# Attention and experts in one Trainium2 kernel: V loaded per quad, K's copy on VectorE, score steps in halves, one PV group per quad, gate by one matmul

## Chip, cores, metric

The kernel runs on one core of one Trainium2 chip. The metric is the device time in microseconds, median of the runs. On one core a run counts as slow when it is over 1.5% above the fastest run of the same kernel. A **ratio** below is the mean time of one kernel's fast runs over the mean of the other's fast runs of the same rounds on the same chip, with a 95% interval, so it is not quite the ratio of the medians quoted beside it.

## The reference, cut

```
q, k, v: [8 batches, 8 heads, 576, 64]   f: [8, 8, 576]
scores = q k^T / 8 + decay from cumsum(log f), causal
x = softmax(scores) v                     -> [8, 576, 512]
e = argmax(mean_over_positions(x) @ w_gate)          # one expert per batch
out = gate * (relu(x @ w1[e]) @ w2[e])               # w1, w2 fp32 in memory, 2 MB each per expert
```

## The kernel before

Four heads of a batch are a **quad** (16 quads), and a quad's scores are made in four **slots**. A slot is one call of `stage_s`: matmuls into four banks of PSUM, the memory that matmuls write (one bank per head), one exponential on ScalarE (ACT) over all four, and a mask on GpSimd (POOL). `stage_pv` makes row sums (`r_ps`) and outputs (`o_ps`), and VectorE (DVE) scales them into `xT`. Reading a result out of PSUM, which frees its tile for the next matmuls, is called an **eviction** below. When both quads of a batch are done, `stage_gate` picks the expert, `stage_weights` loads its weights from POOL's queue, and the expert matmuls are fed in between the slots by `moe(...)`. They start at slot 14. Every engine works through its instructions in the order they are written here.

```
ps_s: one tile [P, 4, 512] fp32 (4 PSUM banks);  ps_w: 4 tiles of one bank, shared by
row sums, outputs, gate and both expert stages

def stage_t(g, j):                       # j = 0: Q, 1: K
    nc.vector.transpose(TR[j], RAW...)
    if j == 0: nc.vector.tensor_copy(dst, src)
    else:      nc.gpsimd.tensor_copy(...)          # K's copy on POOL
def stage_s(g, k):
    ps = ps_s.tile([P, 4, 512], fp32, name="s_ps")
    ... matmuls of 4 heads (4 row groups of the array) into ps[:, j, ...]
    nc.scalar.activation(E[:, :, 0:WIDTH[k]], ps[:, :, 0:WIDTH[k]], AF.Exp, scale=0.125)
    ... nc.gpsimd.affine_select(...)               # mask
def stage_pv(g, blk):                    # 3 tiles of ps_w: r_ps, o_ps, o_ps
    ...
    if n == 1 and blk == 1: nc.vector.tensor_add(pt, pooled[:, :, 0], pooled[:, :, 1])
def stage_gate(b):
    for m in range(4):
        nc.tensor.matmul(lg_ps, pt[:, m:m + 1].to_broadcast([P, P]), wg[:, m, :], start=(m == 0), stop=(m == 3))
    ... logits, max, index, exponential
# ... cut ...
for t in range(4 * NQ + 2):
    g, k4 = divmod(t, 4)
    if g < NQ: stage_s(g, k4)
    # ... t == 0 cut
    if k4 == 0:   moe(t, 0.5); stage_pv(g - 1, 1); ... load_v(batch g // 2 + 1); moe(t, 0.5)
    elif k4 == 1: stage_v(g + 1); stage_t(g + 1, 0); moe(t, 1.0); stage_gate; stage_weights; moe(t, 1.2)
    elif k4 == 2: moe(t, 1.0); stage_pv(g, 0); stage_t(g + 1, 1); moe(t, 0.9)
    else:         load_qk(g + 3, ...); moe(t, 2.4)
```

The softmax here doesn't subtract the row's maximum and nothing guards it: scores larger than these inputs give would overflow.

## Time and profile before

| | before |
|---|---|
| median of 3 runs | 264.78 us (263.08 to 269.06; the last counts as slow) |
| span of the profiled run | 261.2 us |
| first score matmul | 11.35 us |
| first expert matmul | 56.1 us |
| last matmul ends | 255.6 us |

From the page: busy share of each engine, and the granted clock of the matmul engine (PE) in tenths, in 40 slices of 6.5 us.

```profile
PE 224.3 (86%) x3202; PEld 151.7 (58%) x3218; DVE 126.8 (49%) x352; ACT 155.3 (59%) x216; POOL 131.0 (50%) x166
...
PE   6256565569999898999999999999999999999991
...
PEclk9655557579999999999999999999999999999999
```

The clock is at 0.5 to 0.7 from the second to the ninth slice (about 6 to 59 us) and full after that. The same cut by the two borders of the table (columns: stretch, its length, busy time of PE, weight loads, VectorE, ScalarE, POOL, then PE's granted clock, the share of DMA time, GB/s):

```profile
11.35:56.10 44.75, 25.84 (x482) 15.97 (x482) 15.47 (x45) 27.28 (x34) 29.13 (x36) 0.58 0.85 159
56.10:255.60 199.50, 194.20 (x2708) 134.28 (x2724) 104.82 (x290) 125.70 (x180) 97.44 (x120) 0.99 0.84 182
```

I call 11.35 to 56.1 us the **fill** and 56.1 to 255.6 the **full part**. In the fill no engine is busy for more than about two thirds of the time. In the full part PE is busy 194.2 of 199.5 us, so every microsecond of PE work or of PE waiting there is a microsecond of the kernel. Who PE waited for, whole run (total us, times, longest):

```profile
PE s_ps L177 <- POOL kt L169: 14.4, 8, 5.6
PE s_ps L177 <- ACT E L184: 10.7, 11, 2.0
```

The two large waits are nearly all in the fill (12.8 and 10.2 us of them): K's copy on POOL, and the exponential that must empty the four score banks first. And the gate's matmuls, from the costliest groups (busy us, mean ns):

```profile
L241 PE MATMUL logits_ps<-wg,pooledT 128*128 128x8 f32 x64 | 7.8, 248 | 0.4 <-DVE pooledT L234 0.2
```

Their 64 records are eight gates; merged in time each gate keeps PE for 0.8 to 1.0 us.

### The profile page before, as it was taken

Reading aid. Unit: us, or ns where it says so; the run is one execution under the profiler, and the core shown is the slowest. Engines: PE = TensorE matmul, PEld = TensorE weight load, DVE = VectorE, ACT = ScalarE, POOL = GpSimd, SP = SyncE. Lnnn points to the kernel's source line nnn. Section 1 sums busy time; section 2 is a strip of 40 time slices with the busy share of each in tenths; the row PEclk is TensorE's granted clock in tenths of the full one; section 3 lists DMA queues with packets and bytes.
Section 4 is the critical chain, followed back from the end, with each engine's and each line's share of the span. In section 5 each row is a group of like instructions: output and inputs, shape, how many; then the busy total and the mean of one; then the engine's idle time right before and its main releaser. Section 6 shows DMA issues by size and latency. Waiting matters only on the chain.

```text
span 261.2 us, 7676 instructions
## 1 busy us (share of the span) xinstructions
PE 224.3 (86%) x3202; PEld 151.7 (58%) x3218; DVE 126.8 (49%) x352; ACT 155.3 (59%) x216; POOL 131.0 (50%) x166
## 2 busy tenths in 40 slices
PE   6256565569999898999999999999999999999991
PEld 2133333337855684578656865587548755976940
DVE  4551325035645564556554645565646534544430
ACT  3175648357756876678667876688568864430500
POOL 4389564854576557374856584758545621100000
PEclk9655557579999999999999999999999999999999
DMA  6998932999369998999699989999990594299132
GB/s 131 227 231 148 197 52 54 212 218 174 75 123 242 251 229 142 224 277 231 105 229 244 250 159 224 267 218 163 224 262 26 93 221 153 52 191 244 62 101 89
DMA packets 51865, 45.82 MB, mean 175 GB/s; under 512 B 39344, under 2 KB 40624, under 8 KB 50800
## 3 DMA queue, kind: packets, MB, share of 16 engines
q0 software_dynamic: 7936, 26.22, 53.8%
q1 hardware_dynamic: 43456, 18.39, 28.1%
q8 instruction: 27, 0.44, 0.7%
q10 hardware_dynamic: 432, 0.66, 0.7%
q14 instruction: 14, 0.11, 0.1%
HBM read 62.03 MB, written 9.44 MB: 274 GB/s over the span
## 4 chain that ended last, share of the span: by engine, by line
PE 51%; ACT 14%; DVE 12%; DMA 8%; POOL 7%; issue 6%; POOLq 0%; SPq 0%; ACTq 0%; DVEq 0%
PE h_ps L277 17%; PE out_ps L292 16%; ACT E L184 9%; PE s_ps L177 7%; PE o_ps L220 5%; DMA w1e<-in_moe_w_dram 4%; POOL kt L169 4%; DVE tr L162 4%; DMA out_dram<-otile 3%; PE r_ps L220 3%; PE out_ps L305 3%; DVE xT L228 2%; POOL vb L155 2%; ACT ri L226 2%; ACT h1T L283 1%
## 5 line engine op out<-in xcount | busy, mean ns | idle before, releaser
L184 ACT ACTIVATE E<-s_ps 128x1536 bf16<-128x1536 f32 x64 | 96.2, 1503 | 48.8 <-PE s_ps L177 47.8
L277 PE MATMUL h_ps<-xT,w1e 128*128 128x288 bf16 x512 | 73.7, 292 | 2.2 <-ACT h1T L283 1.1
L277 PEld LDWEIGHTS <-w1e 128*128 128x128 bf16 x512 | 62.5, 146 | 9.1 <-issue 5.9
L228 DVE SCALAR_TENSOR_TENSOR xT<-o_ps,ri 128x256 bf16<-128x256 f32 (+1 forms) x64 | 27.0, 456 | 66.9 <-ACT ri L226 59.8
L177 PE MATMUL s_ps<-qt,kt 32*128 32x320 bf16 (+4 forms) x896 | 37.7, 281 | 25.0 <-POOL kt L169 14.4
L292 PE MATMUL out_ps<-w2e,h1T 128*128 128x512 bf16 x240 | 57.9, 380 | 1.0 <-issue 0.3
L283 ACT ACTIVATE h1T<-h_ps,gate_b 128x288 bf16<-128x288 f32 x64 | 31.8, 497 | 27.3 <-PE h_ps L277 27.3
L177 PEld LDWEIGHTS <-kt 32*128 32x128 bf16 x896 | 19.9, 97 | 44.8 <-issue 20.5
L196 POOL TENSOR_SCALAR_AFFINE_SELECT E<-E 128x512 bf16<-128x512 bf16 x32 | 20.8, 649 | 43.2 <-ACT E L184 43.1
L155 POOL TENSOR_TENSOR vb<-vf,WF 128x1024 bf16<-128x1024 f32 (+1 forms) x32 | 40.5, 1266 | 1.3
L292 PEld LDWEIGHTS <-h1T 128*128 128x128 bf16 x256 | 23.2, 98 | 28.9 <-issue 3.5
L280 DVE TENSOR_SCALAR h1T<-h_ps,gate_b 128x288 bf16<-128x288 f32 x64 | 31.8, 508 | 14.4 <-PE h_ps L277 14.4
L299 DVE COPY otile<-out_ps 128x512 f32<-128x512 f32 x31 | 21.3, 688 | 27.2 <-PE out_ps L292 26.7
L220 PE MATMUL o_ps<-E,vb 128*32 128x320 bf16 (+4 forms) x896 | 31.6, 286 | 0.0
L169 POOL COPY kt<-tr 128x576 f32<-128x576 f32 x16 | 20.2, 1260 | 20.5 <-DVE tr L162 19.4
L187 POOL TENSOR_SCALAR_AFFINE_SELECT E<-E 128x1024 bf16<-128x1024 bf16 x16 | 17.4, 1089 | 15.1 <-ACT E L184 15.1
L162 DVE STREAM_TRANSPOSE tr<-raw 128x576 f32<-128x576 f32 x32 | 24.7, 772 | 0.0
L220 PEld LDWEIGHTS <-vb 128*32 128x32 bf16 x896 | 21.8, 107 | 4.5
L220 PE MATMUL r_ps<-E,WB 128*32 128x320 bf16 (+4 forms) x448 | 19.2, 289 | 0.9 <-POOL E L196 0.9
L224 ACT ACTIVATE lr<-r_ps 128x256 f32<-128x256 f32 (+1 forms) x32 | 13.1, 410 | 7.5 <-PE r_ps L220 7.4
L220 PEld LDWEIGHTS <-WB 128*32 128x32 bf16 x448 | 9.6, 100 | 9.7 <-issue 6.3
L226 ACT ACTIVATE ri<-lr 128x256 f32<-128x256 f32 (+1 forms) x32 | 14.2, 445 | 1.0
(52 smaller groups left out, 115.1 us busy)
## 6 DMA issues: line engine op xcount, KB each, us to landing
vf<-in_v_dram SPq DMA_DIRECT2D x32, 256.0 KB, 7.7
w1e<-in_moe_w_dram POOLq DMA_DIRECT2D x8, 1024.0 KB, 8.2
w2e<-in_moe_w_dram POOLq DMA_DIRECT2D x8, 1024.0 KB, 13.4
out_dram<-otile SPq DMA_DIRECT2D x29, 256.0 KB, 6.8
raw<-in_q_dram POOLq DMA_DIRECT2D x16, 288.0 KB, 6.7
raw<-in_k_dram POOLq DMA_DIRECT2D x16, 288.0 KB, 7.8
vf<-in_v_dram SPq DMA_DIRECT2D x8, 128.0 KB, 6.9
out_dram<-otile SPq DMA_DIRECT2D x16, 64.0 KB, 7.5
```

The source lines that it names most:

```text
L155: nc.gpsimd.tensor_tensor(VB[g % NV][p0:P, c0:c1, :, :], VF[b % 2][p0:P, c0:c1, h, :], WF[p0:P, b, c0:c1, h].unsqueeze(3).to_broadcast([P ...
L162: nc.vector.transpose(TR[j], RAW[g % NRAW][:, j, :, :].rearrange("p r e -> p (r e)").bitcast(fp32))
L169: nc.gpsimd.tensor_copy(dst.rearrange("p i r -> p r i"), TR[j].rearrange("p (r i) -> p r i", r=18))
L177: nc.tensor.matmul(ps[:, j, at:at + hi - lo], KT[g % 2][32 * j:32 * j + 32, KLO[c]:KLO[c] + P, a], QT[g % 2][32 * j:32 * j + 32, lo:hi, a] ...
L184: nc.scalar.activation(E[:, :, 0:WIDTH[k]], ps[:, :, 0:WIDTH[k]], AF.Exp, scale=0.125)
L220: nc.tensor.matmul(ps[32 * j:32 * j + 32, lo - i0:w], lhs, E[:, j, at:at + i1 - lo], start=(m == 0), stop=(m == len(segs) - 1))
L228: nc.vector.scalar_tensor_tensor(xT[:, 2 * n + what - 1, i0:i1], ps[:, 0:w], LN_SCALE, ri[:, 0:w], op0=ALU.mult, op1=ALU.mult, accum_out=p ...
L277: nc.tensor.matmul(p1[:, 0:288], w1e[:, m, s:FH:8], xT[:, m, s0:s0 + 288], start=(m == 0), stop=(m == 3))
L280: nc.vector.tensor_scalar(h1T[:, s, s0:s0 + 288], p1[:, 0:288], gate_b[:, 0:1], 0.0, op0=ALU.mult, op1=ALU.max)
L283: nc.scalar.activation(h1T[:, s, s0:s0 + 288], p1[:, 0:288], AF.Relu, scale=gate_b[:, 0:1])
L292: nc.tensor.matmul(p2, h1T[:, hb, s0:s0 + 128], w2e[:, hb, :], start=(hb == 0), stop=(hb == 7))
L299: nc.vector.tensor_copy(otile, p2)
```

## The change

The intent: shorten the fill, and take work off PE in the full part. It loads V per quad instead of per batch; copies K on VectorE and issues the transposes earlier; in the first 14 slots (`FILL`) splits a score step into two halves of two heads, so that one half's exponential can run beside the other half's matmuls; adds two dummy matmuls per slot there to hold the clock up; joins the two PV blocks into one group per quad; makes the gate by a product and a sum on VectorE and one matmul; moves the cumulative sum's tail to POOL. Core of the diff, cuts marked:

```
+    FILL = 14
+    SPS = ps_s.tile([P, 4, 512], fp32, name="s_ps")          # one tile for the whole run
# ... V tiles and loads per quad, cumulative sum on gpsimd: cut ...
-        if j == 0:
-            nc.vector.tensor_copy(dst, src)
-        else:
-            nc.gpsimd.tensor_copy(...)
+        nc.vector.tensor_copy(dst, src)
     def stage_s(g, k):
-        ps = ps_s.tile([P, 4, 512], fp32, name="s_ps")
-        ...
-        nc.scalar.activation(E[:, :, 0:WIDTH[k]], ps[:, :, 0:WIDTH[k]], AF.Exp, scale=0.125)
+        for heads in (((0, 1), (2, 3)) if 4 * g + k < FILL else ((0, 1, 2, 3),)):
+            ... matmuls of these heads into SPS[:, j, at:at + hi - lo]
+            h = slice(heads[0], heads[-1] + 1)
+            nc.scalar.activation(E[:, h, 0:w], SPS[:, h, 0:w], AF.Exp, scale=0.125)
-    def stage_pv(g, blk):
+    def stage_pv(parts):
+        for what, g, blk in [(0, g, blk) for g, blk in parts] + [(w, g, blk) for g, blk in parts for w in (1, 2)]:
     def stage_gate(b):
-        for m in range(4):
-            nc.tensor.matmul(lg_ps, pt[:, m:m + 1].to_broadcast([P, P]), wg[:, m, :], ...)
+        nc.vector.tensor_tensor(prod, wg..., pt..., op=ALU.mult)
+        nc.vector.tensor_reduce(part, prod, axis=X, op=ALU.add)
+        nc.tensor.matmul(lg_ps, ones, part)
# the loop, new order inside a slot:
+        if parts and not fill: stage_pv(parts)                # slot 1: (g-1, 1) and (g, 0)
+        if gate and not fill:  stage_gate(...); stage_weights(...)      # slot 2
+        if g < NQ: stage_s(g, k4)
+        if gate and fill:      stage_gate(...); stage_weights(...)
+        if g < NQ: stage_mask(g, k4)
+        if parts and fill:     stage_pv(parts)
+        # slot 1: stage_t(g+1, 0), load_v(g+2);  slot 2: load_qk(g+3), stage_v(g+1), stage_t(g+1, 1)
+        moe(t, (1.4, 2.2, 2.2, 2.1)[k4])
+        if fill: busy(2)                                       # dummy matmuls
```

## The prediction

> **What bounds it now.** By the windows view the kernel has two parts. From 12 to 56 us (score steps before the first expert matmul) PE is busy about 57% at a granted clock near 0.5; no engine is full there (ACT about 62%). From 70 to 213 us PE is busy 138.2 of 143 us at clock 1.00: PE-bound, with only 4.8 us of idle left. The tail (213 to 255) is pure expert matmul, also full, then about 6 us for the last store.
>
> In the fill a quad takes about 12.5 us. The chain of waits shows why it is serial: scores (0.85 us) then one exponential over four PSUM banks (1.24 to 1.88 us), each waiting for the other; xT, then the K transpose on DVE (0.77), then K's copy on POOL (1.26), and only then the next quad's scores. The timeline of POOL shows that copy queued behind V scaling (2.59 us) and masks; PE waits 2.9 to 4.3 us for it at 35.2 and 48.7 us. The first expert index is ready at about 41.7 us, but POOL issues the weight load at 45.67, after a mask and V scaling; w1e lands 10.4 us later and expert work starts at 56.1.
>
> **Costed.**
> - K's copy on DVE: about 0.7 us instead of 1.26 on POOL, both transposes emitted a slot or more earlier. Removes the waits of 2.9 to 5.6 us at quad starts in the fill; in the full part only 0.2 to 0.3 us per quad. DVE +10 us, POOL -20 us; neither is full. The Trainium skill ("SBUF — State Buffer", shared port pair) says VectorE and GpSimd exclude each other in some modes; the trace agrees (one Q copy took 1.56 instead of 0.65 us beside V scaling), so a few copies will be long.
> - Half steps: exponentials cost about 0.165 us + 0.84 ns per element (from 1.24, 1.45, 1.88 us), so a quad's rise from 6.0 to 6.7 us of ACT; with 1.7 us for Ln/Exp of the sums, 8.4 us if ACT never waits. I estimate 9.3 us per quad, as the six-tile PV group in four PSUM buffers waits for Ln on ACT.
> - Dummy matmuls keep PE warm. The skill ("TensorE: Matmul & The Clock Gate", Part 1) gives half clock when idle, full after about 3.4 us of activity; the trace agrees (0.50 in 20 to 36 us, 1.00 once full).
> - Start: CUM to POOL, transposes earlier: about 1 us.
> - Weights now precede mask and V scaling on POOL. I place the first weight issue at about 38.5 us, landing at 47 to 48; slot 14 is reached at about 43, so PE waits some 4 us for w1e. The expert phase starts at about 48 instead of 56: **-8 us**, all critical since the rest is PE-bound.
> - Gate: eight fp32 matmuls, 0.79 to 1.03 us, become one, about 0.2: **-4.5 us** over seven gates in the PE-bound part.
> - PV group in the full part: PE work unchanged. The second row-sum needs exp plus mask of a step issued only about 2.2 us before (1.45+1.09 needed), and the gate's matmul follows late DVE work: 0 to 0.7 us stall per quad, against present waits that vanish: net **+1 us**. Warmer clock at hand-over: **-1 us**.
>
> Sum about -13 to -14 us: **251 us, range 243 to 258**. Faster by over 2% 0.90, within 2% 0.08, slower 0.02.
>
> **Signs.** Right: first h_ps near 48 us, clock above 0.8 in the fill, ACT over 80% busy there, no PE wait for K's copy, gate matmul near 0.2 us, 25 to 25.5 us per batch in the full part.
>
> **Wrong if** w1e lands late (DMA contention), the fill's clock stays 0.5 (half steps use two of four row groups, so PE would bind), or the PV group stalls PE each quad.

## More of the kernel before

The kernel before was run again with every group of experiments: its medians there were 263.85, 263.94, 264.33, 263.78 and 263.65 us.

The whole scores of the first slot on PE (start, length, engine, line, operation, out<-in, count, and in brackets the idle time before it with what ended it):

```profile
11.35 0.83 PE L177 MATMUL s_ps<-qt,kt 32*128 32x256 bf16 x16 [5.65 <-POOL kt L169]
```

## The result, and the profile after

The change makes the kernel slower: 287.62 us median of 3 runs (286.36 to 287.68) against 264.78; ratio 1.088, interval 1.078 to 1.099. The prediction, a gain of 13 to 14 us to 251 us, was wrong in sign.

| | before | after | difference |
|---|---|---|---|
| to first score matmul | 11.35 | 12.4 | +1.1 |
| fill, to first expert matmul | 44.75 | 60.2 | +15.4 |
| full part, to last matmul | 199.5 | 205.4 | +5.9 |
| last matmul to end | 5.6 | 6.2 | +0.6 |
| span | 261.2 | 284.2 | +23.0 |

The lines of the page that answer to those of before:

```profile
PE 242.3 (85%) x3198; PEld 154.4 (54%) x3198; DVE 140.4 (49%) x383; ACT 158.7 (56%) x227; POOL 116.7 (41%) x153
...
PE   7278776878998999999898989898989899997991
...
PEclk9755586655999999999999999999999999999999
```

PE is now busy 18 us **longer**, and the clock is no better. The windows:

```profile
12.40:72.60 60.20, 45.84 (x523) 21.04 (x522) 18.12 (x55) 30.24 (x46) 22.59 (x29) 0.59 0.61 116
72.60:278.00 205.40, 190.40 (x2670) 131.13 (x2658) 116.39 (x315) 126.13 (x178) 85.42 (x108) 1.00 0.82 177
```

The fill contains 45.8 us of PE work instead of 25.8: 11.9 us are the dummies, 11.1 us come from the scores (22.6 instead of 11.5 us): the 8 matmuls of a half step keep PE for 0.82 us where the 16 of a whole step took 0.83, and the halves come one after the other. In the full part PE works 3.8 us less, as intended (the gate), but sits idle 15.0 us instead of 5.3. Who it waits for:

```profile
PE s_ps L181 <- ACT E L187: 15.4, 22, 1.2
PE r_ps L228 <- POOL E L193: 5.2, 8, 1.0
...
PE logits_ps L254 <- DVE part L253: 4.3, 5, 1.0
PE h_ps L290 <- DMA w1e<-in_moe_w_dram: 1.6, 1, 1.6
```

K's copy has gone from the list, as predicted. In its place: the scores wait for the exponential 22 times instead of 11, the row sums for POOL's mask, and the gate's one matmul for its own sum on VectorE. The gate's line shows its PE time has shrunk as hoped (16 records, two per gate, where there were eight):

```profile
L254 PE MATMUL logits_ps<-part,ones 128*128 128x8 f32 x16 | 3.0, 261 | 5.5 <-DVE part L253 4.3 <-ACT h1T L296 1.1
```

The first look at the fill is the timeline of PE:

```profile
12.42 0.82 PE L181 MATMUL s_ps<-qt,kt 32*128 32x256 bf16 x8
14.14 0.82 PE L181 MATMUL s_ps<-qt,kt 32*128 32x256 bf16 x8 [0.91 <-ACT E L187]
```

and of ScalarE beside it:

```profile
13.28 0.81 ACT L187 ACTIVATE E<-s_ps 128x768 bf16<-128x768 f32 x1 [0.25 <-PE s_ps L181]
15.00 0.81 ACT L187 ACTIVATE E<-s_ps 128x768 bf16<-128x768 f32 x1 [0.91 <-PE s_ps L181]
16.93 1.02 ACT L187 ACTIVATE E<-s_ps 128x1024 bf16<-128x1024 f32 x1 [1.12 <-PE s_ps L181]
19.08 1.02 ACT L187 ACTIVATE E<-s_ps 128x1024 bf16<-128x1024 f32 x1 [1.12 <-PE s_ps L181]
```

Read the two together. The first half's scores start at 12.42, its exponential runs 13.28 to 14.09, and the *second* half's scores start at 14.14: they waited 0.91 us for the exponential of the first half, though they write two other banks. Its own exponential follows at 15.00. So a slot is scores, exponential, scores, exponential, one after the other. Scores and exponentials do not overlap, and each of the four is paid for.

### The profile page after: what moved, and what is told of

It is laid out like the page before. It is cut to its first block, busy times and chain, and to the rows that moved or that the text cites. A ratio compares the mean times of both kernels' runs of the same rounds, so it can differ in the third digit from the quotient of the medians.

```text
span 284.2 us, 7747 instructions
## 1 busy us (share of the span) xinstructions
PE 242.3 (85%) x3198; PEld 154.4 (54%) x3198; DVE 140.4 (49%) x383; ACT 158.7 (56%) x227; POOL 116.7 (41%) x153
## 4 chain that ended last, share of the span: by engine, by line
PE 46%; POOL 14%; ACT 13%; DVE 12%; issue 7%; DMA 4%; POOLq 1%; ACTq 0%; DVEq 0%
PE h_ps L290 16%; PE s_ps L181 11%; ACT E L187 11%; PE o_ps L228 6%; POOL vb L158 5%; PE r_ps L228 4%; PE out_ps L305 4%; POOL E L193 3%; DVE xT L236 3%; DMA w1e<-in_moe_w_dram 3%; PE still_ps L105 3%; DVE tr L165 2%; DVE h1T L293 2%; DVE qt L169 2%; POOL raw L83 1%
## 5 line engine op out<-in xcount | busy, mean ns | idle before, releaser
L187 ACT ACTIVATE E<-s_ps 128x1536 bf16<-128x1536 f32 (+3 forms) x78 | 98.6, 1264 | 59.6 <-PE s_ps L181 58.1
L290 PE MATMUL h_ps<-xT,w1e 128*128 128x288 bf16 x512 | 69.4, 289 | 2.6 <-DMA w1e<-in_moe_w_dram 1.6
L181 PE MATMUL s_ps<-qt,kt 32*128 32x320 bf16 (+4 forms) x896 | 48.7, 282 | 15.5 <-ACT E L187 15.4
L305 PE MATMUL out_ps<-w2e,h1T 128*128 128x512 bf16 x256 | 59.8, 380 | 0.0
L181 PEld LDWEIGHTS <-kt 32*128 32x128 bf16 x896 | 24.4, 97 | 46.8 <-issue 41.1
L158 POOL TENSOR_TENSOR vb<-vf,WF 128x1024 bf16<-128x1024 f32 (+1 forms) x30 | 37.9, 1264 | 1.4
L228 PE MATMUL o_ps<-E,vb 128*32 128x320 bf16 (+4 forms) x896 | 28.7, 284 | 0.0
L276 POOL DMA_DIRECT2D w1e<-in_moe_w_dram x8 | 7.1, 883 | 33.2 <-DVE gate_b L267 18.1
L228 PEld LDWEIGHTS <-WB 128*32 128x32 bf16 x448 | 10.6, 102 | 15.1 <-issue 12.6
L105 PE MATMUL still_ps<-still 128*128 128x512 bf16 x40 | 17.2, 552 | 1.4 <-DVE still L100 1.4
```

The lines of the kernel that those rows point to most:

```text
L105: nc.tensor.matmul(ps, still[:, 0:P], still)
L158: (eng or nc.gpsimd).tensor_tensor(VB[g % NV][p0:P, c0:c1, :, :], VF[g % NF][p0:P, c0:c1, :, :], WF[p0:P, b, c0:c1, h].unsqueeze(3).to_bro ...
L181: nc.tensor.matmul(SPS[:, j, at:at + hi - lo], KT[g % 2][32 * j:32 * j + 32, KLO[c]:KLO[c] + P, a], QT[g % 2][32 * j:32 * j + 32, lo:hi, a ...
L187: nc.scalar.activation(E[:, h, 0:w], SPS[:, h, 0:w], AF.Exp, scale=0.125)
L228: nc.tensor.matmul(ps[32 * j:32 * j + 32, lo - i0:w], lhs, E[:, j, at:at + i1 - lo], start=(m == 0), stop=(m == len(segs) - 1))
L290: nc.tensor.matmul(p1[:, 0:288], w1e[:, m, s:FH:8], xT[:, m, s0:s0 + 288], start=(m == 0), stop=(m == 3))
```

## The experiments

The theory after this reading: (A) the fill lost its time because both halves live in one PSUM tile, and the program makes every writer of a tile wait for the last reader of that tile; (B) the full part lost it to new in-order waits of PE. Rivals: dummies and half clock set the fill; the per-quad V loads, the late expert weights or the six-tile PV group do; the full part's waits only take up slack. The instruction list of the compiled program supports A before any run: in the first step the first matmul of the second half carries a wait for the first half's exponential in the change, and carries none in e1; in later steps of e1 each half waits for the exponential of the same half one step before.

The runs came in five groups of one chip session each. All kernels gave the correct result. "fill ends" is the start of the first expert matmul in the profiled run; the last column is the ratio to the kernel before of the same session.

| run | edit, on what | us | fill ends | ratio to before (95%) |
|---|---|---|---|---|
| e1_two_tiles | after: a PSUM tile per half | 268.82 | 56.0 | 1.018 (1.014 to 1.022) |
| e2_whole | after: no halves | 270.36 | 57.9 | 1.026 (1.022 to 1.030) |
| e3_no_dummies | after: no dummies | 285.02 | 70.3 | 1.084 (1.079 to 1.090) |
| e4_full_part | after: PV order, gate after expert work | 311.29 | 74.4 | 1.179 (1.174 to 1.184) |
| e5_v_early | e1: V scaled a slot earlier | 267.28 | 51.3 | 1.013 (1.006 to 1.020) |
| e6_t_late | e5: Q transpose behind the gate | 271.78 | 51.7 | 1.033 (1.028 to 1.038) |
| e7_cum_dve | e6: cumulative sum on VectorE | 272.36 | 50.7 | 1.033 (1.028 to 1.038) |
| e8_gate_alone | before: gate by one matmul | 275.53 (all four runs) | 57.1 | 1.036 (1.026 to 1.046) |
| e9_gate_early | e8 with the product early | 266.72 | 56.9 | 1.009 (1.005 to 1.012) |
| e10_k_dve | before: K's copy on VectorE | 266.76 | 57.0 | 1.009 (1.006 to 1.013) |
| e11_before_plus | before: e9, e10, halves in two tiles | 268.85 | 57.8 | 1.014 (1.009 to 1.020) |
| e12_repaired | e5: product early, PV order | 260.25 | 50.6 | 0.984 (0.981 to 0.987) |
| e13_t_spread | e12: transposes in slots 2 and 3 | 258.17 | 51.7 | 0.979 (0.975 to 0.983) |
| e14_gate_four | e12: gate undone | 262.00 | 50.3 | 0.993 (0.988 to 0.997) |
| e15_no_dummies2 | e12: no dummies | 263.06 | 52.8 | 1.001 (0.992 to 1.009) |
| e16_whole2 | e12: no halves | 264.30 | 55.1 | 1.001 (0.996 to 1.006) |
| e17_t_spread_full | e13, but fill as e12 | 258.88 | 50.9 | 0.981 (0.978 to 0.983) |
| e18_plus_cum | e17: cumulative sum on VectorE | 259.33 | 51.9 | 0.984 (0.982 to 0.986) |

The intervals of e12, e13, e14, e17 and e18 lie below 1.

### e1_two_tiles and e2_whole: the shared tile

e1:

```
-    SPS = ps_s.tile([P, 4, 512], fp32, name="s_ps")
+    HALF = [ps_h.tile([P, 2, 512], fp32, name=f"s_ps{i}") for i in range(2)]   # until slot 14
+    # at slot 14 the pool ps_h is closed and one tile [P, 4, 512] opened
```

> The two halves of a fill step get a PSUM tile of their own each; nothing else changes. Theory (the halves share one tile, so the second half's scores wait for the first half's exponential, and score and exponential never overlap): the wait of 0.6 to 1.1 us between the exponentials inside a step vanishes, about 0.9 us in each of 14 steps, so the first expert matmul comes at 58 to 61 us instead of 72.6 and the time falls by 11 to 14 us, to about 275. Rival (half clock and dummy matmuls on PE set the fill): first expert matmul stays within 3 us of 72.6.

e2:

```
-        for heads in (((0, 1), (2, 3)) if 4 * g + k < FILL else ((0, 1, 2, 3),)):
+        for heads in ((0, 1, 2, 3),):
```

> Fill steps whole again (one exponential over all four heads), all the rest of the change kept. Theory (halves in series are what lengthened the fill): scores in the fill take half the PE time (about 11.5 us of it instead of 22.6), one wait per step instead of two, first expert matmul at 58 to 61 us, time 274 to 277. Rival (dummies, six-tile PV group or late weights set the fill): above 282.

Both bring back 17 to 19 us of the 23: 268.82 and 270.36 us, fill ending at 56.0 and 57.9 instead of 72.6. PE in e1 for the first slot, and ScalarE for the same two slots (x2 means two merged instructions with no gap between them):

```profile
12.22 0.84 PE L189 MATMUL s_ps<-qt,kt 32*128 32x256 bf16 x16
```

```profile
13.08 1.51 ACT L195 ACTIVATE E<-s_ps 128x768 bf16<-128x768 f32 x2 [0.25 <-PE s_ps L189]
15.04 1.94 ACT L195 ACTIVATE E<-s_ps 128x1024 bf16<-128x1024 f32 x2 [0.44 <-PE s_ps L189]
```

The 0.91 us gap inside the step is gone: the two exponentials follow each other without a pause, since the second half's scores were made beside the first half's: all 16 matmuls of the slot take 0.84 us, against 0.83 in the kernel before. Over the fill the scores keep PE for 14.7 us instead of 22.6. Theory A holds, and the rivals (dummies, clock, PV group, weight load) fall for the size of the loss, as all of these are still in e1 and e2. That e1's clock in the fill is 0.70 instead of 0.59 is a consequence. The Trainium skill ("PSUM — Partial Sum Buffer", section "PSUM bank collisions raise a hardware error") asks for a guard per bank and quadrant, and says that accesses to different banks run clean; the halves are in different banks, and e1 ran correctly without that wait, which agrees. So the wait was the program's tracking by tile, not the hardware's need.

The miss in both: they gained more than expected (18.8 and 17.3 us against 11 to 14 and 10 to 14). The expectation of e1 counted one gap of about 0.9 us per step where ScalarE's lines show two, 0.91 us inside the first step and 1.12 before the next. Over the fill ScalarE waited 25.6 us for scores in the change (26 times), 8.3 in e1 (10 times) and 11.3 in e2 (12 times).

### e3_no_dummies

```
-        if fill:
-            busy(2)
```

> Dummy matmuls of the fill (28 of them, 11.9 us of PE) left out, halves kept. Theory: they run beside the second half's exponential, which lasts about as long, so the time changes by less than 3 us, down if at all. Rival (dummies hold the scores back): the fill shrinks by 8 to 12 us. If they keep the clock up, the fill gets longer instead.

285.02 us, 2.6 less than the change's 287.62 (of another session; the ratios are 1.084 and 1.088, whose intervals overlap). The rival, 8 to 12 us, falls. The dummies cost little in the serial fill, since they run beside the second half's exponential (14.89 to 15.92 us beside 15.00 to 15.81 in the first slot). Nor did they hold its clock up: 0.57 without them, 0.59 with them.

### e4_full_part: a repair that made it worse

```
-        for what, g, blk in [all row sums first, then all outputs]
+        for what, g, blk in [(w, g, blk) for g, blk in parts for w in (0, 1, 2)]
-        if gate and not fill: stage_gate; stage_weights      # before the slot's stage_s
         moe(...)
+        if gate and not fill: stage_gate; stage_weights      # behind the slot's expert work
```

> Only the full part: row sum, then outputs of the first block, then row sum and outputs of the second; and the gate after the slot's expert work instead of before it. Theory (two new in-order waits cost the full part about 10 us of PE: second row sum for the mask 5.2, gate matmul for its product 4.3 to 5.4): both waits fall below 1.5 us each and the time falls by 6 to 10 us, to 278 to 281. Rival (they only take up slack): within 2 us of 287.

311.29 us: 24 us slower, where 6 to 10 less were expected. The first half of the edit did what it should (no wait of row sums for masks is left in its list), but the gate's wait grew from 4.3 to 16.4 us in eight gates. VectorE at one gate, and POOL at the same time:

```profile
91.36 1.75 DVE L250 TENSOR_TENSOR prod<-wg,pooledT 128x32 f32<-128x32 f32 x1
93.14 0.19 DVE L253 TENSOR_REDUCE part<-prod 128x8 f32<-128x32 f32 x1
```

```profile
91.13 2.60 POOL L158 TENSOR_TENSOR vb<-vf,WF 128x1024 bf16<-128x1024 f32 x2
```

The product, 0.2 us elsewhere (median 198 ns in the change), took 1.75 us: it reads two tensors from SBUF, and POOL had begun to scale V 0.2 us earlier. The Trainium skill ("SBUF — State Buffer", section "SBUF: two separate sides") says that a VectorE instruction with two SBUF inputs and a GpSimd instruction exclude each other for a whole instruction; the trace agrees with it here, as the product ended at 93.11 and the first of POOL's two instructions at 93.05. PE waited 2.7 us for it, and what followed ran at half clock (third column from the right is the clock):

```profile
90.00:93.00 3.00, 0.71 (x4) 0.10 (x1) 2.25 (x2) 0.00 (x0) 2.98 (x3) 1.00 0.70 93
93.00:95.00 2.00, 1.62 (x12) 0.81 (x13) 0.90 (x7) 0.27 (x2) 0.65 (x2) 0.54 1.04 179
95.00:98.00 3.00, 3.00 (x8) 0.87 (x6) 0.16 (x1) 1.24 (x3) 1.95 (x3) 0.50 0.72 141
98.00:101.00 3.00, 3.00 (x25) 1.27 (x24) 0.69 (x1) 1.45 (x1) 0.45 (x1) 0.67 0.95 177
```

So a late operand cost twice: the wait, and some 6 us of slow matmuls behind it. PE's busy time rose by 12 us though its work was the same. The weights, which are loaded behind the gate, came later too: PE waited 8.0 us for `w1e` instead of 1.6, 6.5 of it once. The edit moved two things at once, and the verdict on each rests on its own waits, not on the time.

### e5_v_early, e6_t_late, e7_cum_dve: order on POOL and VectorE

e5 (on e1):

```
-        if k4 == 2 and g + 1 < NQ: stage_v(g + 1)
+        if k4 == 1 and g + 1 < NQ: stage_v(g + 1)
```

> e1_two_tiles with V scaled on POOL one slot earlier (slot 1 of a quad, behind that slot's mask), so that it no longer stands ahead of the masks that the PV group waits for. Theory (row sums wait for masks that stand behind V scaling and Q/K load issues on POOL): the waits of row sums for masks, 8.4 us in e1, fall below 2 us, the clock holds in quads 2 and 3 of the fill; first expert matmul 3 to 5 us earlier (51 to 53 us), time 6 to 10 us below e1, 259 to 263. Rival (the wait is for the exponential, not for the mask's place in the queue): r_ps still waits 5 us or more, time within 3 us of e1.

The fill ended at 51.3 instead of 56.0, as expected, but the time fell by 1.5 us only, and the ratios 1.018 and 1.013 have intervals that overlap. The row sums' wait fell from 8.4 to 4.2 us, not below 2; the gate's rose from 5.9 to 9.4. The 4.7 us won in the fill were given back in the full part.

e6 (on e5):

```
-        if k4 == 1 and 1 <= g and g + 1 < NQ: stage_t(g + 1, 0)
         if k4 == 2 and 1 <= g and g + 1 < NQ:
+            stage_t(g + 1, 0)
             stage_t(g + 1, 1)
```

> e5 with the Q transpose and copy (1.4 us of DVE) moved behind the gate's DVE work. Theory (the gate's matmul holds PE in order until DVE has gone through transposes and evictions): wait of the gate's matmul, 5.9 us in e1, falls to 1 to 2 us, time 4 to 6 us below e5. Rival (wait comes from evictions, or the product is held by POOL): less than 2 us gained.

A miss: 4.5 us slower. The gate still waited 8.5 us, and its lines at one gate show that the transposes were not what it waited for there:

```profile
64.14 0.52 DVE L301 TENSOR_SCALAR h1T<-h_ps,gate_b 128x288 bf16<-128x288 f32 x1 [0.46 <-PE h_ps L298]
64.58 0.64 DVE L258 TENSOR_TENSOR prod<-wg,pooledT 128x32 f32<-128x32 f32 x1
```

```profile
65.49 0.39 PE L262 MATMUL logits_ps<-part,ones 128*128 128x8 f32 x2 [0.90 <-DVE part L261]
```

The product stands in VectorE's order behind the eviction of the expert matmuls that PE did last, so PE cannot have its gate operand until its own last work has been read out, 0.9 us later at this gate, wherever the transposes stand. It also took 0.64 us (median) instead of 0.2, at this gate beside a mask on POOL that began at 64.54. The two transposes in one slot now held up the expert evictions: expert matmuls waited 7.2 us for them instead of 3.5.

e7 (on e6): the five `nc.gpsimd` lines of the cumulative sum back to `nc.vector`.

> e6 with the five operations on the cumulative sum back on VectorE (POOL took 2.2 to 2.6 and 1.6 to 2.0 us for the two large ones, VectorE 0.51 and 0.45). Theory: first scores at 10 to 10.5 us instead of 12.2, time 1.5 to 2.5 us below e6. Rival (first scores wait for the Q/K load instead): no gain.

The first scores came 1.7 us earlier (10.7 instead of 12.4), the time did not move (272.36 against 271.78). The rival in its second part held: scores wait for K, 5.2 us instead of 2.7.

### e8_gate_alone and e9_gate_early: the gate by itself

e8, on the kernel before: the change's `stage_gate` alone.

> The kernel before with one part of the change alone: gate by a product and a sum on VectorE and one matmul. Theory (in the PE-bound part every gate saves PE 0.5 to 0.65 us, if pooled sums are ready long before): 3 to 4.5 us faster than before, ratio 0.984 to 0.989, no wait of the gate's matmul over 0.3 us. Rival (the two more VectorE operations make PE wait as they did in the change): within 1 us of before.

The expected saving of 3 to 4.5 us is a loss: ratio 1.036 of the fast runs (275.06 and 271.25 us; two further runs, 276.0 and 276.2, fell under the 1.5% rule for slow, and the profile is of one of these; the clock of all four was alike, 0.904 to 0.915). PE waits 13.8 us for the gate's sum, up to 2.0 us each, where it waited 0.2 in all before. One gate:

```profile
97.24 0.16 DVE L236 TENSOR_TENSOR pooledT<-pooled 128x4 f32<-128x4 f32 x1
97.33 0.77 DVE L164 STREAM_TRANSPOSE tr<-raw 128x576 f32<-128x576 f32 x1
98.13 0.65 DVE L169 COPY qt<-tr 128x576 f32<-128x576 f32 x1
98.69 0.52 DVE L286 TENSOR_SCALAR h1T<-h_ps,gate_b 128x288 bf16<-128x288 f32 x1
99.12 0.47 DVE L243 TENSOR_TENSOR prod<-wg,pooledT 128x32 f32<-128x32 f32 x1
99.62 0.19 DVE L246 TENSOR_REDUCE part<-prod 128x8 f32<-128x32 f32 x1
```

```profile
99.96 0.36 PE L247 MATMUL logits_ps<-part,ones 128*128 128x8 f32 x2 [1.97 <-DVE part L246]
```

The pooled sum is ready at 97.40. Before, the gate's matmuls read it directly and could start there. Now they need a product and a sum that VectorE does only after a transpose, a copy and an expert eviction, at 99.62: the matmul is shorter, but its operand comes 2 us later.

e9 puts the two operations right behind the pooled sum:

```
             nc.vector.tensor_add(pt, pooled[:, :, 0], pooled[:, :, 1])
+            nc.vector.tensor_tensor(prod, wg..., pt..., op=ALU.mult)
+            nc.vector.tensor_reduce(part, prod, ...)
     def stage_gate(b):
+        nc.tensor.matmul(lg_ps, ones, part)
```

> The kernel before with the gate by one matmul, as in e8, but its product and sum stand on VectorE right behind the pooled sum, ahead of the transposes. Theory (e8 was slow since PE, in order, waited up to 2.0 us per gate for a product queued behind the transposes, 13.8 us in all, and the clock fell to half after such a gap): the gate's matmul waits less than 2 us in all, 3 to 5 us faster than before, 259 to 261. Rival (the form itself, a product and sum on VectorE, is what costs): slower than before by 2 us or more.

The gate's wait is gone (1.2 us in all) and PE's gate time falls from 7.8 to 2.6 us. And still it is 0.9% *slower* than before. Neither theory had that. The list of waits shows where the saving went:

```profile
PE h_ps L283 <- DVE h1T L286: 6.2, 6, 1.1
...
PE logits_ps L247 <- DVE part L241: 1.2, 2, 0.6
```

PE, done with the gate sooner, reaches the expert matmuls sooner and waits there 6.2 us for VectorE to empty a PSUM tile; in the kernel before that wait does not appear. VectorE has the product and the sum, a transpose and a copy ahead of the eviction at this point; that the longer gate had been covering this queue I infer. PE's account nearly closes: 5.2 us saved on the gate stand against 6.2 us of new waits for evictions and 1.0 more for the gate, a loss of 2.0 of the 2.4 us. Why the evictions come later than the gate's saving alone would make them was not tested; VectorE is 3.2 us busier (130.0 against 126.8).

### e10_k_dve and e11_before_plus: parts of the change on the kernel before

e10: `nc.vector.tensor_copy(dst, src)` for K as well, alone.

> The kernel before with K's copy on VectorE instead of POOL, alone. Theory (in the fill PE waits 12.8 us for that copy, which stands behind V scaling and masks on POOL): that wait falls by 6 us or more, first expert matmul at 48 to 51 us instead of 56.1, time 4 to 8 us less, 256 to 260. Rival (the K chain only hides the exponentials and the weight load): first expert matmul within 2 us of 56, time within 2 us of before.

The rival held: fill ends at 57.0, ratio 1.009. PE's wait for K fell only from 14.4 to 9.4 us, since VectorE's queue had it instead of POOL's, and a wait of 3.3 us for the scaled V appeared. K's copy was the last link that the list of waits named, with others right behind it.

e11: e9, e10, and the halves with a tile each, on the kernel before.

> The kernel before plus three parts of the change, mended: gate as in e9, K's copy on VectorE as in e10, half steps in the fill with a PSUM tile for each half. Theory (each part gains if it puts no new wait on PE): the gains of e9 and e10 add and halves give 1 to 3 us more; first expert matmul at 46 to 50 us, time 250 to 256. Rival (weight load bounds the hand-over): first expert matmul not before 50 us and no more than e9 and e10 give together.

A miss: 268.85 us, fill ends at 57.8. In the old order of slots the gate and K's copy do not pay alone, nor the three parts together (halves alone were not run on the kernel before): expert matmuls wait 8.0 us for evictions, scores 8.8 us for K.

### e12_repaired: the change with its waits mended

On e5: product and sum right behind the pooled sum (as e9), and each block's outputs right behind its own row sum (as in e4).

> The change with its waits mended: e5 plus the gate's product and sum ahead of the transposes, and each block's outputs right behind its own row sum. Theory (the full part's loss is the gate's wait, 9.4 us in e5, and the row sums' wait for masks, 4.2): both fall below 2 us, time 254 to 258. Rival (the one PV group per quad or per-quad V loads cost by themselves): above 262.

260.25 us, ratio 0.984, interval 0.981 to 0.987: 1.6% below the kernel before. Against the change that is about 27 us. Against e5, from which only the two edits differ, the ratio falls from 1.013 to 0.984 while the fill's end moves by 0.7 us: this is what shows theory B, for the two waits together and not for each. The waits are nearly gone, the time stays 2 us above what was expected. PE's list:

```profile
PE h_ps L298 <- DVE h1T L301: 4.4, 8, 0.8
PE o_ps L236 <- DVE xT L244: 3.5, 12, 0.7
PE logits_ps L262 <- DVE h1T L301: 2.8, 4, 0.7
PE s_ps L189 <- ACT E L195: 2.3, 10, 0.3
```

No row sum waits for a mask. What is left in the full part is mostly waits for PSUM tiles that VectorE empties.

```profile
12.40:50.50 38.10, 32.44 (x519) 16.94 (x522) 18.10 (x53) 28.33 (x46) 25.08 (x31) 0.79 0.93 177
50.50:252.00 201.50, 187.69 (x2656) 130.27 (x2661) 123.52 (x317) 127.01 (x178) 85.04 (x107) 1.00 0.84 182
```

The fill is 6.7 us shorter than before (38.1 against 44.75, the clock 0.79 against 0.58). The full part holds 6.5 us less PE work and lasts 2.0 us longer (201.5 against 199.5): idle went from 5.3 to 13.8 us. (Some matmul records are missing from the traces: 19 of 3198 in e12, where about 1 us of the idle has no other cause, 16 in the kernel before, none in the change.)

### e13 to e16: what each part is worth once mended

e13 (on e12): `stage_t(g + 1, 0)` in slot 2 and `stage_t(g + 1, 1)` in slot 3.

> e12 with the Q transpose in slot 2 and the K transpose in slot 3 of a quad instead of 1 and 2. Theory (in the full part PE waits for PSUM buffers because VectorE has transposes queued between the PV evictions and the expert evictions; 4.4 us of h_ps and 2.8 us of the gate's matmul wait for h1T in e12): these waits fall to 3 us together or less, time 2 to 5 us below e12, 255 to 258. Rival (evictions wait for ACT or for PE itself): within 1 us of e12, or K comes too late for the next quad and it is slower.

258.17 us, ratio 0.979 against e12's 0.984, at the low end of the expected gain; the two sessions' intervals overlap slightly (0.975 to 0.983, 0.981 to 0.987), so the gain is likely rather than shown. The waits for evictions fell as expected, from 7.2 to 0.3 us, and two others came up:

```profile
PE s_ps L189 <- DVE kt L171: 5.3, 5, 2.2
...
PE h_ps L298 <- DMA w1e<-in_moe_w_dram: 3.3, 5, 1.4
...
PE h_ps L298 <- DVE h1T L301: 0.3, 1, 0.3
```

e14 (on e12): four matmuls on the pooled sum again, no product.

> e12 with the gate undone: four fp32 matmuls on the pooled sum, no product and sum on VectorE. Theory (what one matmul saves on PE, about 0.6 us a gate, is handed back as a wait for VectorE's evictions, as in e9): PE 4 to 5 us busier, waits for h1T smaller by about as much, time within 2 us of e12. Rival (the saving is real once the product is early): 3 to 5 us slower than e12.

Ratio 0.993 against 0.984, so the one-matmul gate, with its operand early, is worth about 0.9% or 2.2 us here. On PE the gate takes 8.2 us in e14 and 2.8 in e12, so of 5.4 us saved some 3 are handed back as waits (for `h1T` 7.2 us in e12, 4.8 in e14), which is the theory; but not all of it.

e15 (on e12): no dummies.

> e12 without the dummy matmuls of the fill. If they hold the clock up: clock in 15 to 45 us falls towards 0.5 and the first expert matmul comes 2 to 5 us later than 50.6. If they only stand in the way: 1 to 3 us earlier. I lean to the first; in e12 the clock there was 0.5 to 0.9.

Ratio 1.001 against 0.984: without the dummies the gain is gone, or nearly (by the medians the loss is 2.8 us; one run of 266.37 widens the interval to 0.992 to 1.009). In 12 to 45 us the clock is 0.60 instead of 0.81 (e12 first, then e15), and the fill ends 2.2 us later, 52.8 against 50.6.

```profile
12.00:45.00 33.00, 27.61 (x413) 13.95 (x417) 16.66 (x46) 24.79 (x40) 20.82 (x27) 0.81 0.90 169
12.00:45.00 33.00, 22.52 (x368) 13.63 (x366) 16.69 (x46) 23.61 (x38) 18.91 (x23) 0.60 0.87 164
```

e16 (on e12): whole steps.

> e12 with whole steps in the fill (one tile). Theory (mended half steps overlap scores with exponentials and are worth about 0.5 us a step at most): first expert matmul 2 to 6 us later than 50.6, time 2 to 6 us above e12. Rival (gate and weight load bound the hand-over, e1 against e2 differed by 1.5 us only): within 2 us of e12.

Ratio 1.001 against 0.984, fill ends at 55.1: mended half steps are worth about 4.5 us, within the theory's range.

### e17_t_spread_full and e18_plus_cum

e17: e13's order from the fourth quad on, e12's in the fill. e18: e17 with the cumulative sum on VectorE.

> e13 with the transposes in slots 2 and 3 only from the fourth quad on; in the fill they stay in slots 1 and 2 as in e12. Theory (e13's 2.2 us wait for K in the fill is from its late slot there): that wait vanishes and the time is 1 to 3 us below e13, about 256; ratio to before 0.968 to 0.976. Rival: the wait in the fill moves to another engine and the ratio stays at 0.979.

> e17 with the cumulative sum's five operations on VectorE. Theory (PE starts its first scores 1 to 2 us earlier, and the fill is a chain from there): 1 to 2 us below e17. Rival (as in e7 against e6, which gained nothing): within 1 us of e17, the gain being lost to the wait for the next quad's K or the V load.

Neither gains: 0.981 and 0.984 against e13's 0.979, with overlapping intervals for e13 and e17. In e18 the first scores come at 10.5 instead of 12.4, and the wait of scores for K rises from 4.6 to 8.6 us, as e7 had shown. The best version stays e13, with e17 no different within the intervals.

## Why the prediction was wrong, point by point

- **"Half steps: … I estimate 9.3 us per quad"** is the step that failed. It took for granted that one half's scores overlap the other half's exponential. In the change they do not: both halves share one tile and run in series, and the quads of the fill take 16.0 and 17.2 us (scores of slot 0 at 27.8, 43.8 and 61.0 us). With a tile each (e1) the second quad took 9.4 us, with ScalarE busy 8.1 of them, so the sum fits the program that I had thought I read in that quad; the third and the fourth took 13.8 and 10.7 us. The evidence was in the diff, in the one line that hoists a single `SPS` tile out of the steps.
- **"The expert phase starts at about 48 instead of 56: -8 us."** It started at 72.6. Mended, it starts at 50.6 (e12), 5.5 us before the kernel before's. In e1, with the halves mended, the third quad took 13.8 us instead of 9.3: row sums waited for masks that stood behind V scaling on POOL, and PE for the gate, which the estimate had not counted, and the clock was 0.78 instead of 0.99.
- **"Gate: … -4.5 us."** Wrong as a gain. PE's time for it did fall (7.8 to about 3 us), but the term counted only work on PE and not when its operand would be ready. By itself the gate cost 3.6% (e8); with the operand early 0.9% (e9), the saving turned into a wait for evictions; only in the mended change is it worth 2.2 us (e14).
- **"PV group … net +1 us."** The mechanism was right and was named: the second row sum needs a mask that has not come, and the gate's matmul follows late VectorE work. The size was not: 5.2 and 4.3 to 5.4 us, against some 2 us that vanished. The full part had 9.7 us more idle time on PE; e12, with both waits mended, shows what they cost together (ratio 1.013 in e5, 0.984 in e12).
- **"Dummy matmuls keep PE warm"**: right where the scores are not serial (e15: clock 0.60 without, 0.81 with, and 1.7% of the time); of no use in the change, whose clock in the fill was 0.59 with them and 0.57 without (e3). The Trainium skill ("TensorE: Matmul & The Clock Gate", Part 1) gives about 3.4 us of sustained activity as what releases full clock, and the trace agrees with the direction only: with more PE work in the same 33 us (27.6 us against 22.5) the clock was higher. The 3.4 us no run here shows, and in the 20 to 36 us that the prediction named PE was at 0.50 while busy for 8.6 of the 16 us, not idle.
- **K's copy on VectorE**: the wait on POOL did vanish, as predicted, but by itself it bought nothing (e10): scores then waited 9.4 us for the same copy on VectorE, and outputs 3.3 us for the scaled V.
- **"Start: CUM to POOL … about 1 us"** had the wrong sign. POOL took 2.58 and 1.64 us for the two large operations that VectorE does in 0.51 and 0.45, so the first scores, which the change puts behind the transposes of the cumulative sum on PE, came 1.1 us later. It did not matter: taking it back gained nothing (e7, e18).
- **What I had named as making it wrong** (late w1e, half clock, PV group) was partly there: clock 0.59, PV stalls of 5.2 us. The one that counted was not on the list. Of the signs, only the vanished wait for K's copy came: ScalarE was busy 30.2 of 60.2 us in the fill instead of over 80%, a gate kept PE for about 0.4 us instead of 0.2, and a batch in the full part took 27.7 to 28.7 us from gate to gate (but for the last) instead of 25 to 25.5.

What stays open: why e9's evictions come so late, what each of the full part's two repairs is worth alone, and whether per-quad V loads are worth anything by themselves; no run undid them alone.

## What to carry to other kernels

Splitting a step to overlap two engines gains nothing unless the two halves are separate for whatever tracks the dependencies: give each half its own tile, and look in the trace whether the second half really starts before the first one is read. On an engine that is full and works in order, the cost of an operation is also when its operand is ready, not only how long it runs; here a shorter matmul behind a longer queue on another engine was a loss. And when a wait is removed, ask what stood right behind it: here the same microseconds came back as waits for masks, for evictions and for K.

## What the Trainium skill lacked or had wrong

- No page has it: two matmul groups that write different banks of one PSUM tile were made to wait for a reader of the other banks. "PSUM — Partial Sum Buffer" gives the hardware's unit (bank and quadrant), but nothing warns that a program's guard can be as wide as the tile. Here it cost 18.8 us of 288 (medians of after and e1, of two sessions; ratios to before 1.088 and 1.018).
- "TensorE: Matmul & The Clock Gate", the table in "Why this matters for your kernels", asks for no idle gaps over about 3 us. Shorter gaps were enough here: in e4 the one of 2.7 us was followed by a clock of 0.50 to 0.67 over the next 8 us, and all four others of 2.7 us by a fall to about 0.5 too; in e8 three of six gaps of 1.9 to 2.0 us in the full part were followed by one, and three were not. Gaps of about 1 us in the change left it at 1.00 from 83 to 250 us.
- "GPSIMD Engine Reference", section 4.1, has elementwise work with one input run at about line rate on GpSimd. Here a 64x576 fp32 minimum with a constant took 1.64 us on GpSimd with VectorE idle (after) and 1.96 in e1, against 0.45 us on VectorE, and two operations in one instruction 2.23 to 2.58 (with copies of VectorE beside them) against 0.51 us.
